# A transformer block on one core: a gate vector folded by copies, and another order for the first loads

## The chip, the cores and the metric

The kernel runs on one core of a Trainium2 chip. The metric is the device time of one execution in microseconds (us). The profile is of one execution, recorded by the hardware. In it PE is TensorE's matmul, PEld its weight load, DVE is VectorE, ACT is ScalarE, POOL is GpSimd and SP is SyncE, which here only issues DMA transfers. A q after an engine's name (SPq, ACTq) means its queue of DMA issues.

## The reference

One block of a diffusion transformer, with B = 2 sequences of N = 256 tokens, D = 1152 features and F = 4608, all in bf16. There are two heads.

```python
mod = (silu(c) @ w_mod).reshape(B, 6, 1, D)
shift_a, scale_a, gate_a, shift_m, scale_m, gate_m = [mod[:, i] for i in range(6)]
h = layernorm(x) * (1 + scale_a) + shift_a
q, k, v = split(h @ wqkv)                    # two heads of 576
a = softmax(q @ k.T * 576 ** -0.5) @ v @ wo
x = x + gate_a * a
h2 = layernorm(x) * (1 + scale_m) + shift_m
return x + gate_m * (gelu(h2 @ w_fc1) @ w_fc2)
```

## The kernel before

The 512 tokens are four tiles of 128 (t = 0 to 3). All weights are streamed from HBM in the order of their use, by SyncE. The start is a relay: c and x come in, `silu(c)` gives `sT`, x gets its statistics (ScalarE sums tiles 0 and 2, VectorE takes 1 and 3), and the normalized x is transposed on TensorE. The scale of the modulation is computed in five groups of feature blocks, each as soon as its columns of `w_mod` are there, and K is accumulated one feature block (`k_step`) at a time behind it.

```python
x_sb = act.tile([P, NT, D], BF16, name="x_sb", tag="x_sb")
nc.scalar.dma_start(c_sb[:], c_v)
nc.scalar.dma_start(touch_x[:], x_v[:, 1, 0, 0:32])
for t in (0, 1, 3, 2):
    nc.sync.dma_start(x_sb[:, t, :], x_v[:, t // TPB, t % TPB, :])
# ... constants ...
SGROUPS = [(0, 2), (2, 4), (4, 6), (6, 8), (8, 9)]
KM1 = 6

def load_k(k0, k1, c0, c1):
    nc.sync.dma_start(w_k[:, k0:k1, c0:c1], wqkv_v[:, k0:k1, D + c0:D + c1])

for k0, k1 in SGROUPS:
    nc.sync.dma_start(w_scale_a[:, :, k0 * P:k1 * P],
                      wmod_v[:, :, S_SCALE_A * D + k0 * P:S_SCALE_A * D + k1 * P])
    for a, z in [(0, 1), (1, 2)] if k0 == 0 else [(k0, k1)]:
        load_k(a, z, 0, KM1 * P)
load_k(0, KD, KM1 * P, D)
# ... then w_shift_a in two parts between the rows of w_q, w_gate_a, w_v, w_o ...
```

A scale group of two blocks is 18 narrow matmuls (128x2). The middle of the K accumulation is this loop. `transpose_x` puts block k + 1 of the normalized x into PSUM, and `both` multiplies it by the scale, the first sequence on VectorE and the second on ScalarE, into `hT0`:

```python
def both(pt, k):
    for b, e in enumerate("da"):
        modulate(pt, 0, k, b, b * N, e)

for k in range(3, KD):
    split = 2 if k in (3, 5) else 0
    k_step(k, 0, T, 0, split)              # matmuls m = 0 .. split-1 of block k
    if k in (3, 5, 7):
        k1 = min(k + 3, KD)
        scale_add(scale_group(k + 1, k1), k + 1, k1)
    if k < KD - 1:
        both(transpose_x([k + 1], range(NT)), k + 1)
    k_step(k, 0, T, split)                 # the rest of the six
```

After K come its last three panels, `shift_a` (`vec_section`), Q, the scores, V, the attention, the output projection, the second norm, the two MLP products. The last gate vector, `gate_m`, is computed on VectorE beside the first product: `part` gathers, in each of 128 partitions, the products of nine rows of `w_gate_m` with `silu(c)`. The 128 partitions must then be summed. VectorE transposes 32x32 blocks and sums them into `folded` (128 x 2 x 36). In it the four groups of 32 partitions are still separate, and the kernel before adds them with a matmul against `fold`, a matrix of four stacked identities:

```python
fold = const.tile([P, 32], FP32, name="fold")
nc.vector.tensor_reduce(fold[:], ident[:].rearrange("p (q a) -> p a q", a=32), axis=AX.X, op=ALU.add)

def gate_vector_finish(g, folded):
    rows = D // 32
    pg = aux_tile([rows, B, 32], "pg")
    for b in range(B):
        nc.tensor.matmul(pg[:, b, :], folded[:, b, :], fold[:], start=True, stop=True)
    nat = work.tile([rows, B, 32], BF16, name="nat_v", tag="nat_v", bufs=1)
    nc.vector.tensor_copy(nat[:], pg[:])
    for b in range(B):
        nc.gpsimd.dma_start(gates_dram[g, b, :].rearrange("(j r) -> j r", r=32), nat[:, b, :])
    return broadcast_gate(g)      # DRAM -> all 128 partitions, GpSimd's queue

# in the first MLP product, m = 12 .. 35, nine matmuls each
    if m == 22:
        gate_m_finish = gate_vector(1, w_gate_m)
    if m == KF - 2:
        gate_m = gate_m_finish()
```

Its first use is behind the first group of the second product, `tmp = pacc * gate_m`, whose accumulators come from a pool of six.

Of the kernel before, what the change touches and what calls it, by code (L numbers as in the profile page):

```python
# [8 lines left out]
FP32 = mybir.dt.float32  # L9
BF16 = mybir.dt.bfloat16  # L10
ACT = mybir.ActivationFunctionType
ALU = mybir.AluOpType
AX = mybir.AxisListType
# [6 lines left out]
def kernel(  # L20
# [11 lines left out]
    nc = tc.nc  # L32
    B, N, D = x.shape
# [3 lines left out]
    P = 128  # L37
    T = B * N
    NT = T // P
    TPB = N // P  # L40
    KD = D // P
    KF = F // P
# [7 lines left out]
    WAIT_FOR = mybir.DependencyInfo(mybir.DependencyClass.Sync, mybir.DependencyReason.DATA)  # L50
    first_traced = len(nc.cur_bb.bb.instructions)

    const = ctx.enter_context(tc.tile_pool(name="const", bufs=1))
    act = ctx.enter_context(tc.tile_pool(name="act", bufs=1))
    wide = ctx.enter_context(tc.tile_pool(name="wide", bufs=5))
    work = ctx.enter_context(tc.tile_pool(name="work", bufs=2))
    small = ctx.enter_context(tc.tile_pool(name="small", bufs=4))
    psum = ctx.enter_context(tc.tile_pool(name="psum", bufs=2, space=PSUM))

    def acc_tile(shape, name, dt=FP32):  # L60
        return psum.tile(shape, dt, name=name, tag="acc", bufs=6)

    def aux_tile(shape, name, dt=FP32):
        return psum.tile(shape, dt, name=name, tag="aux", bufs=2)


    x_v = x.rearrange("b (p l) d -> p b l d", l=TPB)
    out_v = out.rearrange("b (p l) d -> p b l d", l=TPB)
    c_v = c.rearrange("b (k p) -> (b k) p", p=P)
    wqkv_v = wqkv.rearrange("(k p) n -> p k n", p=P)  # L70
# [7 lines left out]
    def wide_tile(name):  # L78
        return wide.tile([P, KD, D], BF16, name=name, tag="wide")


    x_sb = act.tile([P, NT, D], BF16, name="x_sb", tag="x_sb")
# [2 lines left out]
    touch_x = act.tile([P, 32], BF16, name="touch_x")  # L85
    nc.scalar.dma_start(touch_x[:], x_v[:, 1, 0, 0:32])
    for t in (0, 1, 3, 2):
        nc.sync.dma_start(x_sb[:, t, :], x_v[:, t // TPB, t % TPB, :])  # L88

    zeros = const.tile([P, T], BF16, name="zeros")  # L90
    nc.vector.memset(zeros[:], 0.0)
    ident = const.tile([P, P], BF16, name="ident")
# [7 lines left out]
    SGROUPS = [(0, 2), (2, 4), (4, 6), (6, 8), (8, 9)]  # L100
    KM1 = 6
    w_scale_a = wide_tile("w_scale_a")
    w_k = wide_tile("w_k")

    def load_k(k0, k1, c0, c1):
        nc.sync.dma_start(w_k[:, k0:k1, c0:c1], wqkv_v[:, k0:k1, D + c0:D + c1])

    for k0, k1 in SGROUPS:
        nc.sync.dma_start(
            w_scale_a[:, :, k0 * P:k1 * P],  # L110
            wmod_v[:, :, S_SCALE_A * D + k0 * P:S_SCALE_A * D + k1 * P],
        )
        for a, z in [(0, 1), (1, 2)] if k0 == 0 else [(k0, k1)]:
            load_k(a, z, 0, KM1 * P)
    load_k(0, KD, KM1 * P, D)

    first_load = {}

    def load_rows(name, view, col0):
        w = wide_tile(name)  # L120
        for r in range(0, KD, 3):
            load = nc.sync.dma_start(w[:, r:r + 3, :], view[:, r:r + 3, col0:col0 + D])
            first_load.setdefault(name, load.ins)
        return w
# [5 lines left out]
    for (j0, j1), rows in zip(SHG, QROWS):  # L130
# [25 lines left out]
        act_func_set_id=LN_EXP_TABLES, name=nc.get_next_instruction_name(),  # L156
        engine=mybir.EngineType.Activation,
    ))
    neg_half = const.tile([P, B], FP32, name="neg_half")
    nc.gpsimd.memset(neg_half[:], -0.5)  # L160
    early = small.tile([P, 1], FP32, name="early", tag="early", bufs=1)
# [81 lines left out]
    def scale_group(k0, k1, tile_of=aux_tile, pm=None):  # L243
        if pm is None:
            pm = tile_of([P, k1 - k0, B], "pm")
        for j in range(k0, k1):
            if j == 0:
                nc.tensor.matmul(pm[:, 0, :], ones_row[:], ones_row[:, 0:B], start=True, stop=False)
            for k in range(KD):
                nc.tensor.matmul(  # L250
                    pm[:, j - k0, :], w_scale_a[:, k, j * P:(j + 1) * P], sT[:, k, 0:B],
                    start=(k == 0 and j > 0), stop=(k == KD - 1),
                )
        return pm

    def scale_add(pm, k0, k1, eng="d"):
        if eng == "a":
            nc.scalar.activation(scale_a[:, k0:k1, :], pm[:], ACT.Identity, bias=ones[:])
        else:
            nc.vector.tensor_scalar_add(scale_a[:, k0:k1, :], pm[:], 1.0)  # L260

    def transpose_x(ks, ts, pt=None, j0=0):
        if pt is None:
            pt = aux_tile([P, len(ks), len(ts) * P], "pt", BF16)
        for j, t in enumerate(ts, j0):
            for i, k in enumerate(ks):
                nc.tensor.transpose(pt[:, i, j * P:(j + 1) * P], xns[t][:, k * P:(k + 1) * P], ident[:])  # L267
        return pt
# [9 lines left out]
    def k_step(k, c0=0, c1=T, m0=0, m1=KM1):  # L278
        for m in range(m0, m1):
            if k == 0 and c0 == 0:  # L280
                pk[m] = acc_tile([P, T], "pk")
            nc.tensor.matmul(  # L282
                pk[m][:, c0:c1], w_k[:, k, m * P:(m + 1) * P], hT0[:, k, c0:c1],
                start=(k == 0 and c0 == 0), stop=(k == KD - 1), skip_group_check=True,
            )
# [33 lines left out]
# [3 lines that stand above are left out]
# [76 lines left out]
    k_step(2, 0, N)  # L398
    k_step(2, N, T)
    for k in range(3, KD):  # L400
        split = 2 if k in (3, 5) else 0
        k_step(k, 0, T, 0, split)
        if k in (3, 5, 7):
            k1 = min(k + 3, KD)
            scale_add(scale_group(k + 1, k1), k + 1, k1)
        if k < KD - 1:
            both(transpose_x([k + 1], range(NT)), k + 1)
        k_step(k, 0, T, split)
    for m in range(KM1):
        k_evac(m)  # L410

# [38 lines left out]

    s32 = const.tile([P, KD, B], FP32, name="s32")
    nc.vector.tensor_copy(s32[:], sT[:, :, 0:B])
    fold = const.tile([P, 32], FP32, name="fold")
    nc.vector.tensor_reduce(fold[:], ident[:].rearrange("p (q a) -> p a q", a=32), axis=AX.X, op=ALU.add)
    gates_dram = tc.dram_tile([2, B, D], BF16, name="gates_dram")

    def broadcast_gate(g):
        gate = act.tile([P, B, D], BF16, name="gate", tag="gate")
        for b in range(B):
            nc.gpsimd.dma_start(gate[:, b, :], gates_dram[g, b:b + 1, :].partition_broadcast(P))  # L460
        return gate
# [3 lines left out]
    def gate_vector(g, wg):  # L465
        part = act.tile([P, B, D], FP32, name="part", tag="x_sb")
        folded = small.tile([P, B, D // 32], FP32, name="folded", tag="folded", bufs=1)
        for k in range(KD):
            for b in range(B):
                if k == 0:  # L470
                    nc.vector.tensor_scalar_mul(part[:, b, :], wg[:, k, :], s32[:, k, b:b + 1])  # L471
                else:
                    nc.vector.scalar_tensor_tensor(  # L473
                        part[:, b, :], wg[:, k, :], s32[:, k, b:b + 1], part[:, b, :],
                        op0=ALU.mult, op1=ALU.add,
                    )
        for b in range(B):
            for c in range(0, D, PW):
                blocks = work.tile([P, PW // 32, 32], FP32, name="tmp", tag="tmp", bufs=3)
                nc.vector.transpose(blocks[:].rearrange("p j r -> p (j r)"), part[:, b, c:c + PW])  # L480
                nc.vector.tensor_reduce(
                    folded[:, b, c // 32:(c + PW) // 32], blocks[:], axis=AX.X, op=ALU.add
                )

        return lambda: gate_vector_finish(g, folded)

    def gate_vector_finish(g, folded):
        rows = D // 32
        pg = aux_tile([rows, B, 32], "pg")
        for b in range(B):  # L490
            nc.tensor.matmul(pg[:, b, :], folded[:, b, :], fold[:], start=True, stop=True)
        nat = work.tile([rows, B, 32], BF16, name="nat_v", tag="nat_v", bufs=1)
        nc.vector.tensor_copy(nat[:], pg[:])  # L493
        for b in range(B):
            nc.gpsimd.dma_start(gates_dram[g, b, :].rearrange("(j r) -> j r", r=32), nat[:, b, :])  # L495
        return broadcast_gate(g)

    def gate_natural(g, wg):
# [130 lines left out]
    w_gate_m = load_rows("w_gate_m", wmod_v, S_GATE_M * D)  # L629
# [118 lines left out]
    def f1_mm(dst, m, k, c0, c1, start, **kw):  # L748
        ml = m % KD
        nc.tensor.matmul(  # L750
            dst, w_f1[m // KD][:, k, ml * P:(ml + 1) * P], hT[:, k, c0:c1],
            start=start, stop=(k == KD - 1), **kw,
        )
# [23 lines left out]
    gate_m = None  # L777
    for m in range(MSPLIT, KF):
        pacc = acc_tile([P, T], "pacc")
        for k in range(KD):  # L780
            f1_mm(pacc[:], m, k, 0, T, k == 0)
        nc.scalar.activation(gT[:, m, :], pacc[:], ACT.Gelu_apprx_tanh)  # L782
        if m == 22:
            gate_m_finish = gate_vector(1, w_gate_m)
        if m == KF - 2:
            gate_m = gate_m_finish()
        if m == MSPLIT:
            load_f2(0)
        if m > MSPLIT and m % KD == KD - 1:
            load_f2(m // KD)  # L790
# [9 lines left out]
    for gi, (n, t, c0, cw) in enumerate(groups):  # L800
        b = t // TPB
        last = gi == len(groups) - 1
        pacc = acc_tile([P, cw], "pacc")
        for kk in range(KF):
            j, r = divmod(n * KF + kk, 27)
# [3 lines left out]
                start=(kk == 0), stop=(kk == KF - 1),  # L809
# [11 lines left out]
    for ins in list(nc.cur_bb.bb.instructions)[first_traced:]:  # L821
        eng = ins.engine
# [38 lines left out]
```

## Time and profile before

| what | value |
|---|---|
| time, median of three runs | 243.47 us (242.92 to 243.62) |
| span of the profiled execution | 241.3 us |
| PE busy | 236.3 us, 98% |
| PEld busy | 144.6 us, 60% |
| DVE, ACT, POOL busy | 91.6, 60.1, 28.3 us |
| HBM read | 50.15 MB, 213 GB/s over the span |
| the four loads of x, 288 KB each: issue to landing | 2.9, 3.2, 4.6, 5.1 us |
| first scale group, 576 KB: issued at, to landing | 2.57 us, 6.6 us |

The page gives busy time by engine, then the chain of work that ended last, then groups of instructions. A line of the timeline or of the chain begins with its start and its duration in us; then come the engine, the line of the kernel (L282), the operation and the tiles, and in brackets the idle time before it and what ended that. Matmuls are pipelined, so a busy PE is not a PE at its peak, and the idle time of an engine that is not the bottleneck costs nothing.

### The profile page before, as it was taken

The numbers are of one execution on the slowest core, as the hardware profiler recorded it, in microseconds if no ns is written. First come the engines' busy times: TensorE is split into PE (matmuls) and PEld (weight loads), VectorE is DVE, ScalarE is ACT, GpSimd is POOL, SyncE is SP. The second block draws the span as 40 slices with busy tenths as digits, with TensorE's granted clock in tenths as the row PEclk, the third lists the DMA queues.
The fourth block names the chain that finished last, engine by engine and source line by source line (L and its number), as shares of the span: only waits on it lengthen the run. The fifth ranks groups of instructions, "written<-read, shape, count | busy, mean of one in ns | idle before, by whom it ended". The sixth has DMA issues, their size and how long they took to land.

```text
span 241.3 us, 3993 instructions
## 1 busy us (share of the span) xinstructions
PE 236.3 (98%) x1698; PEld 144.6 (60%) x1698; DVE 91.6 (38%) x194; ACT 60.1 (25%) x122; POOL 28.3 (12%) x47
## 2 busy tenths in 40 slices
PE   8899999999999999999999999999999999999994
PEld 5675444466667566888844444444666656666674
DVE  4842442319325678930002999950000000000001
ACT  6732322307215032770423333222000000000000
POOL 2300000001400324100000000001121111111111
PEclk9999999999999999999999999999999999999999
DMA  6999999998599994739999999999300000000000
GB/s 196 324 317 311 376 367 391 389 393 249 99 315 397 387 311 81 196 62 364 390 392 392 339 326 284 285 326 275 98 16 16 20 16 16 19 18 18 26 25 16
DMA packets 48925, 53.30 MB, mean 221 GB/s; under 512 B 9731, under 2 KB 36619, under 8 KB 48907
## 3 DMA queue, kind: packets, MB, share of 16 engines
q1 hardware_dynamic: 41312, 50.14, 62.6%
q10 hardware_dynamic: 7083, 1.72, 4.9%
q0 software_dynamic: 512, 1.19, 2.2%
q8 instruction: 13, 0.21, 0.4%
q14 instruction: 5, 0.04, 0.1%
HBM read 50.15 MB, written 1.19 MB: 213 GB/s over the span
## 4 chain that ended last, share of the span: by engine, by line
PE 95%; DMA 2%; DVE 1%; SPq 0%; issue 0%; DVEq 0%
PE pacc L806 29%; PE pacc L750 29%; PE pacc L697 7%; PE pacc L603 7%; PE pq L525 7%; PE pk L282 5%; PE pk L311 2%; DMA x_sb<-in_x_dram 2%; PE pa L644 2%; PE ps_s L560 2%; PE pn L420 2%; PE pt L267 1%; PE pm L250 1%; DVE stats L195 1%; PE pg L502 0%; SPq L88 0%
## 5 line engine op out<-in xcount | busy, mean ns | idle before, releaser
L750 PE MATMUL pacc<-hT,w_f 128*128 128x256 bf16 (+1 forms) x432 | 70.5, 326 | 0.0
L806 PE MATMUL pacc<-w_f,gT 128*128 128x384 bf16 (+2 forms) x468 | 70.5, 314 | 0.0
L806 PEld LDWEIGHTS <-gT 128*128 128x128 bf16 x468 | 44.4, 98 | 26.2
L750 PEld LDWEIGHTS <-w_f 128*128 128x128 bf16 x432 | 42.2, 98 | 27.6
L812 DVE TENSOR_TENSOR tmp<-pacc,gate 128x384 f32<-128x384 f32 (+2 forms) x13 | 6.9, 527 | 65.6 <-PE pacc L806 57.3
L782 ACT ACTIVATE gT<-pacc 128x512 bf16<-128x512 f32 x24 | 14.3, 597 | 32.7 <-PE pacc L750 32.7
L473 DVE SCALAR_TENSOR_TENSOR part<-w_gate_m,s,part 128x1152 f32<-128x1152 bf16 x16 | 21.4, 1414 | 0.0
L814 POOL TENSOR_TENSOR o_sb<-tmp,x 128x384 bf16<-128x384 f32 (+1 forms) x12 | 11.6, 971 | 53.9 <-DVE tmp L812 53.9
L697 PE MATMUL pacc<-w_o,big 128*128 128x384 bf16 x108 | 17.9, 326 | 0.0
L525 PE MATMUL pq<-hT,w_q 128*128 128x512 bf16 x81 | 17.8, 379 | 0.0
L603 PE MATMUL pacc<-w_v,hT 128*128 128x384 bf16 x108 | 17.7, 326 | 0.0
L603 PEld LDWEIGHTS <-hT 128*128 128x128 bf16 x108 | 10.5, 98 | 7.1 <-issue 0.3
L697 PEld LDWEIGHTS <-big 128*128 128x128 bf16 x108 | 10.4, 98 | 7.2 <-issue 0.4
L525 PEld LDWEIGHTS <-w_q 128*128 128x128 bf16 x81 | 7.9, 98 | 9.4
L282 PE MATMUL pk<-big,w_k 128*128 128x256 bf16 (+1 forms) x72 | 13.2, 325 | 0.0
L703 POOL TENSOR_TENSOR x<-tmp,x_sb 128x384 f32<-128x384 f32 x8 | 7.3, 911 | 26.3 <-DVE tmp L702 26.3
L471 DVE TENSOR_SCALAR part<-w_gate_m,s 128x1152 f32<-128x1152 bf16 x2 | 1.6, 818 | 22.2 <-DMA w_gate_m<-in_w_mod_dram 22.2
L495 POOL DMA_DIRECT2D gates_dram<-nat_v x2 | 1.1, 534 | 67.7 <-DVE nat_v L493 67.7
L282 PEld LDWEIGHTS <-w_k 128*128 128x128 bf16 x72 | 6.8, 97 | 3.5 <-issue 0.2
L771 ACT ACTIVATE gT<-pacc 128x512 bf16<-128x512 f32 x12 | 6.5, 597 | 9.1 <-PE pacc L750 9.1
L516 POOL DMA_DIRECT2D gates_dram<-nat x4 | 2.4, 596 | 49.8 <-DVE nat L513 48.4
L175 PE MATMUL pwarm<-zeros 128*128 128x256 f32 x18 | 6.7, 540 | 1.2 <-DVE eps_t L95 1.2
(106 smaller groups left out, 164.4 us busy)
## 6 DMA issues: line engine op xcount, KB each, us to landing
w_f<-in_w_fc_dram SPq DMA_DIRECT2D x12, 864.0 KB, 14.2
w_f<-in_w_fc_dram SPq DMA_DIRECT2D x3, 1728.0 KB, 10.1
w_f<-in_w_fc_dram SPq DMA_DIRECT2D x2, 2592.0 KB, 17.2
w_gate_a<-in_w_mod_dram SPq DMA_DIRECT2D x3, 864.0 KB, 14.4
w_v<-in_wqkv_dram SPq DMA_DIRECT2D x3, 864.0 KB, 15.4
w_o<-in_wo_dram SPq DMA_DIRECT2D x3, 864.0 KB, 14.7
w_shift_m<-in_w_mod_dram SPq DMA_DIRECT2D x3, 864.0 KB, 9.5
w_scale_m<-in_w_mod_dram SPq DMA_DIRECT2D x3, 864.0 KB, 15.8
```

Source lines behind the costliest of these rows:

```text
L175: nc.tensor.matmul(dst[:, 0:T // 2], zeros32[:, 0:P], zeros32, start=True, stop=True)
L282: nc.tensor.matmul(pk[m][:, c0:c1], w_k[:, k, m * P:(m + 1) * P], hT0[:, k, c0:c1], start=(k == 0 and c0 == 0), stop=(k == KD - 1), skip_g ...
L473: nc.vector.scalar_tensor_tensor(part[:, b, :], wg[:, k, :], s32[:, k, b:b + 1], part[:, b, :], op0=ALU.mult, op1=ALU.add,)
L525: nc.tensor.matmul(pq[m][:], w_q[:, k, m * P:(m + 1) * P], hT[:, k, :], start=(k == 0), stop=(k == KD - 1), skip_group_check=True,)
L603: nc.tensor.matmul(pacc[:], hT[:, k, t * P:(t + 1) * P], w_v[:, k, pnl * PW:(pnl + 1) * PW], start=(k == 0), stop=(k == KD - 1),)
L697: nc.tensor.matmul(pacc[:], aT[:, k, t * P:(t + 1) * P], w_o[:, k, c0:c1], start=(k == 0), stop=(k == KD - 1),)
L703: (nc.gpsimd if pool_add else nc.vector).tensor_tensor(x1[:, t, c0:c1], tmp[:], x_sb[:, t, c0:c1], op=ALU.add)
L750: nc.tensor.matmul(dst, w_f1[m // KD][:, k, ml * P:(ml + 1) * P], hT[:, k, c0:c1], start=start, stop=(k == KD - 1), **kw,)
L782: nc.scalar.activation(gT[:, m, :], pacc[:], ACT.Gelu_apprx_tanh)
L806: nc.tensor.matmul(pacc[:], gT[:, kk, t * P:(t + 1) * P], w_f2[j][:, r, c0 - n * PW:c0 - n * PW + cw], start=(kk == 0), stop=(kk == KF - 1),)
L812: nc.vector.tensor_tensor(tmp[:], pacc[:], gate_m[:, b, c0:c0 + cw], op=ALU.mult)
L814: (nc.vector if last else nc.gpsimd).tensor_tensor(o_sb[:], tmp[:], x1[:, t, c0:c0 + cw], op=ALU.add)
```

## The change

There are four parts. The fold no longer uses TensorE: GpSimd's queue copies the four groups of 32 partitions of `folded` side by side into 32 partitions (`quads`), and VectorE sums, transposes and converts them. So the gate is finished as soon as it is folded and not at the next to last accumulator. In the K accumulation, three matmuls stand ahead of the second and third scale groups in place of two, so that their weights may come later, and the steps of blocks 4 and 6 are taken in halves, one sequence at a time. The first scale group's weights are issued from ScalarE's queue behind its table load, so that they travel beside x and not behind it. And row 0 of the K weights, with all that SyncE issues behind it, is held until the last load of x has landed, so that those rows don't take the DMA engines from x and the scale group.

```diff
@@ loads @@
-        nc.sync.dma_start(x_sb[:, t, :], x_v[:, t // TPB, t % TPB, :])
+        last_x = nc.sync.dma_start(x_sb[:, t, :], x_v[:, t // TPB, t % TPB, :])
...
-        nc.sync.dma_start(w_k[:, k0:k1, c0:c1], wqkv_v[:, k0:k1, D + c0:D + c1])
-
-    for k0, k1 in SGROUPS:
-        nc.sync.dma_start(
+        return nc.sync.dma_start(w_k[:, k0:k1, c0:c1], wqkv_v[:, k0:k1, D + c0:D + c1])
+
+    def load_scale(eng, k0, k1):
+        eng.dma_start(
             w_scale_a[:, :, k0 * P:k1 * P],
             wmod_v[:, :, S_SCALE_A * D + k0 * P:S_SCALE_A * D + k1 * P],
         )
+
+    for k0, k1 in SGROUPS:
+        if k0:
+            load_scale(nc.sync, k0, k1)
         for a, z in [(0, 1), (1, 2)] if k0 == 0 else [(k0, k1)]:
-            load_k(a, z, 0, KM1 * P)
+            load = load_k(a, z, 0, KM1 * P)
+            if a == 0:
+                tc.add_manual_dep(load.ins, last_x.ins.name, WAIT_FOR, reason="x first")
...
         engine=mybir.EngineType.Activation,
     ))                                       # ScalarE's table load
+    load_scale(nc.scalar, *SGROUPS[0])
@@ K accumulation @@
-        split = 2 if k in (3, 5) else 0
+        split = 3 if k in (3, 5) else 0
...
-        k_step(k, 0, T, split)
+        for c0, c1 in ((0, N), (N, T)) if k in (4, 6) else ((0, T),):
+            k_step(k, c0, c1, split)
@@ gate vector @@
-    fold = const.tile([P, 32], FP32, name="fold")
-    nc.vector.tensor_reduce(fold[:], ident[:].rearrange("p (q a) -> p a q", a=32), axis=AX.X, op=ALU.add)
...
-        pg = aux_tile([rows, B, 32], "pg")
-        for b in range(B):
-            nc.tensor.matmul(pg[:, b, :], folded[:, b, :], fold[:], start=True, stop=True)
-        nat = work.tile([rows, B, 32], BF16, name="nat_v", tag="nat_v", bufs=1)
-        nc.vector.tensor_copy(nat[:], pg[:])
-        for b in range(B):
-            nc.gpsimd.dma_start(gates_dram[g, b, :].rearrange("(j r) -> j r", r=32), nat[:, b, :])
+        quads = small.tile([32, P // 32, B * rows], FP32, name="quads", tag="quads", bufs=1)
+        for a in range(P // 32):
+            nc.gpsimd.dma_start(quads[:, a, :], folded[32 * a:32 * (a + 1), :, :].rearrange("p b j -> p (b j)"))
+        total = small.tile([32, 96], FP32, name="total", tag="total", bufs=1)
+        nc.vector.memset(total[:], 0.0)
+        nc.vector.tensor_reduce(
+            total[:, 0:B * rows], quads[:].rearrange("p a c -> p c a"), axis=AX.X, op=ALU.add,
+        )
+        turned = small.tile([32, 96], FP32, name="turned", tag="turned", bufs=1)
+        nc.vector.transpose(turned[:], total[:])
+        nat = small.tile([32, 96], BF16, name="nat_v", tag="nat_v", bufs=1)
+        nc.vector.tensor_copy(nat[:], turned[:])
+        # ... two writes to gates_dram from GpSimd's queue ...
         return broadcast_gate(g)
@@ first MLP product @@
         if m == 22:
-            gate_m_finish = gate_vector(1, w_gate_m)
-        if m == KF - 2:
-            gate_m = gate_m_finish()
+            gate_m = gate_vector(1, w_gate_m)
```

More of the change, by code (lines that the diff above doesn't have):

```diff
@@ L483, in gate_vector @@
                 )
-        return lambda: gate_vector_finish(g, folded)
-    def gate_vector_finish(g, folded):
         rows = D // 32
-        pg = aux_tile([rows, B, 32], "pg")
-        for b in range(B):
-            nc.tensor.matmul(pg[:, b, :], folded[:, b, :], fold[:], start=True, stop=True)
-        nat = work.tile([rows, B, 32], BF16, name="nat_v", tag="nat_v", bufs=1)
-        nc.vector.tensor_copy(nat[:], pg[:])
-        for b in range(B):
-            nc.gpsimd.dma_start(gates_dram[g, b, :].rearrange("(j r) -> j r", r=32), nat[:, b, :])
+        quads = small.tile([32, P // 32, B * rows], FP32, name="quads", tag="quads", bufs=1)
[10 more added lines that the diff above has]
+        nc.vector.tensor_copy(nat[:], turned[:])
+        flat = gates_dram[g, :, :].rearrange("b (j r) -> (b j) r", r=32)
+        nc.gpsimd.dma_start(
+            flat[0:64, :].rearrange("(q c) r -> c q r", q=2), nat[:, 0:64].rearrange("c (q r) -> c q r", q=2),
+        )
+        nc.gpsimd.dma_start(flat[64:B * rows, :], nat[0:B * rows - 64, 64:96])
         return broadcast_gate(g)
```

## The prediction

> **What bounds the kernel now.** I read first the page's busy shares, then the chain of waits that ended last (whole, then cut to the first 35 us), then the timeline of the two stretches that the change touches, then the DMA issues one at a time with their times to landing.
>
> The page says TensorE is busy 98% of the span, and the chain says 95% of the end is set by it. So a change counts only where it removes TensorE work, or where TensorE waits. The first place is the fold of the last gate vector. The chain has it as a piece of its own, between matmuls of the first MLP product:
>
> ```profile
> 97.31 68.26 PE pacc L750 x423
> 165.57 0.26 PE pg L491 x4
> 165.82 2.05 PE pacc L750 x9
> 167.87 70.31 PE pacc L806 x468
> ```
>
> The reader is to see that the four fold matmuls stand in the chain, and that the nine matmuls behind them took 2.05 us. The same stretch on ScalarE shows the rhythm of the accumulators around it:
>
> ```profile
> 163.66 0.60 ACT L782 ACTIVATE gT<-pacc 128x512 bf16<-128x512 f32 x1 [1.34 <-PE pacc L750]
> 165.61 0.60 ACT L782 ACTIVATE gT<-pacc 128x512 bf16<-128x512 f32 x1 [1.35 <-PE pacc L750]
> 167.91 0.60 ACT L782 ACTIVATE gT<-pacc 128x512 bf16<-128x512 f32 x1 [1.71 <-PE pacc L750]
> ```
>
> The first column is the start. One accumulator follows another by 1.95 us (163.66 to 165.61), and the one with the fold in it by 2.30 us.
>
> The second place is the start. Here TensorE waits for x, for the norm, and then runs beside the loads. From the chain of the first 35 us:
>
> ```profile
> 1.63 4.60 DMA x_sb<-in_x_dram
> 6.23 0.02 issue
> 6.25 1.49 DVE stats L195 x3
> ...
> 7.92 0.68 DVE xn L235 x2
> 8.60 0.04 issue
> 8.64 0.62 PE pt L267 x8
> ```
>
> The third of the four loads of x lands at 6.23 us, VectorE takes its statistics at once, normalizes, and TensorE starts its useful work at 8.64. The fourth quarter was issued at 2.06 and took 5.1 us to land, 7.2 us; ScalarE starts its statistics of it at 7.23. So both late quarters of x sit on the path with nothing to spare. What the DMA engines did in this time, in stretches (the last two columns are their busy share and the GB/s):
>
> ```profile
> 0.70:1.70 1.00, 0.52 (x1) 0.50 (x2) 0.28 (x2) 0.00 (x0) 0.82 (x4) 1.00 0.00 0
> 1.70:4.50 2.80, 2.80 (x8) 1.79 (x7) 0.73 (x4) 2.35 (x3) 0.76 (x3) 1.00 0.96 299
> 4.50:6.00 1.50, 1.50 (x5) 1.17 (x4) 1.47 (x4) 1.47 (x3) 0.00 (x0) 1.00 0.84 227
> 6.00:9.00 3.00, 2.30 (x16) 1.72 (x15) 2.65 (x9) 2.73 (x8) 1.30 (x4) 1.00 1.07 325
> ```
>
> For one microsecond after the first issue nothing moves; then the engines are full but for a hole of 16% of 1.5 us at 4.5 to 6.0. After that TensorE and the loads run neck and neck. Two scale groups come just late:
>
> ```profile
> 15.37 0.57 PEld L250 LDWEIGHTS <-w_scale_a 128*128 128x128 bf16 x18 [0.26 <-DMA w_scale_a<-in_w_mod_dram]
> 19.09 0.52 PEld L250 LDWEIGHTS <-w_scale_a 128*128 128x128 bf16 x18 [0.45 <-DMA w_scale_a<-in_w_mod_dram]
> ```
>
> These idle times are of the weight loads. In the chain the second group took 0.56 us where the first two took 0.43, so TensorE itself lost about 0.13 us there, and hardly anything at 15.4. That is all that a smoother supply of scale groups could give.
>
> **What the Trainium skill says.** "DMA: Bandwidth & Descriptors", section "Issuing engines are not separate DMA queues": transfers from several issuing engines run on the same 16 DMA engines and interleave; a second issuer saves only issue time. The trace of before can't show it, since its ScalarE queue carries only two tiny loads there, but its busy share of 0.96 and above says there is little idle time to take. The same page, "Queues, rings and completion order": each DMA engine takes turns between the queues that have work. If so, x and the first scale group share the engines in the changed kernel, where before the group stood behind x in one queue. "Perfetto Trace Analysis", section "Per-instruction lifecycle": the recorded time of a DMA instruction is that of its descriptors and not of the data. Before agrees: x is issued in some 0.4 us a quarter and lands after 2.9 to 5.1. "VectorE: DVE Perf Modes", section "Why `tensor_reduce` can't reduce along partition axis": lanes don't exchange data. That is why the new fold needs copies before its reduction; no run yet shows it.
>
> **The change, part by part.**
>
> Fold by copies. It removes four matmul records (0.26 us) from TensorE's chain, and the nine matmuls behind them stop paying for the switch: 2.05 us against the usual 1.95. Together 2.30 - 1.95 = 0.35, or 0.26 + 0.10 = 0.36. I take -0.36. In their place VectorE and the GpSimd queue do the work. The last block of the vector is folded at 159.86 + 0.55 = 160.4. Four copies are issued at some 0.55 us each (the old writes of the vector took 1.06 for two) to 162.6 and land some 3 us later (the old writes took 3.7 to land), 165.6; four small VectorE operations take about 1 us; the two writes to DRAM another 4.2; the broadcast 4.3. Estimate: the gate is there at about 175, where it came at 174.40. The first output group is finished near 173.3, and with six accumulators of 5.4 us each TensorE can go on for some 30 us without it. So nothing of this shows in the time. The dropped reduction that made the fold matrix (0.36 us of VectorE at 32.8) lies off the path: 0.
>
> Later scale groups and halves. The split of 3 moves one matmul of 0.215 us (0.86 for four) ahead of each of two scale groups: no work more, and 0.2 us more time for the load. It would recover the 0.13, if the loads were as punctual as before. The halves turn 12 matmuls of 512 columns into 24 of 256. The chain has 18 of 256 and two of 512 in 2.41 us, so one of 256 takes (2.41 - 0.43)/18 = 0.110, and a pair 0.220 for 0.215: 12 x 0.005 = +0.06. What they buy is that the first half needs only VectorE's product; it makes up for the matmul that no longer stands between the scale group and this step.
>
> First scale group from ScalarE's queue, row 0 held. The group (576 KB) was issued at 2.57 and landed at 9.17, and TensorE took it at 9.3. So it was just in time, and earlier is worth nothing, as TensorE waits at 8.64 for the norm of x. What it costs: from the moment that its pieces of 512 B flow, they take turns with rows of 2304 B of x, and x has 2304/2816 = 82% of the engines. If they flow from about 3.6 us, x still has 1.18 MB - 1.9 x 0.299 = 0.61 MB to go. It took from 3.6 to 6.2 and 7.2 for its last two quarters; 22% longer is +0.6, less the hole of 0.16 x 1.5 = 0.24 us that it fills. I take +0.35 us on the late quarters of x. These stand on the path, so TensorE starts later, or waits at 11.08 for the last quarter's norm.
>
> Then the hold. Row 0 of K is issued only when x is in, say at 7.55. From the first issue of x to its landing in an empty queue took 2.9 us for 288 KB, so 192 KB should land after some 2.5 us, near 10.05. TensorE took row 0 at 10.13, which becomes about 10.5 with the later x: row 0 makes it. What comes behind is less sure. With 1 us before anything moves, the engines can run dry once x and the first group (1.77 MB) are through, near 7.5, until about 8.5. That is 0.3 MB not moved at 325 GB/s, less 0.08 MB won in the old hole. Much of it is idle time of those DMA engines that had run ahead, and a landing waits for the slowest, so I put the delay of later loads at 0.3 us, which lies beside the +0.35 of x and is not added to it. I take +0.40 for the start, of which the later groups give back 0.05.
>
> Sum: 243.47 - 0.36 + 0.06 + 0.40 - 0.05 = 243.52.
>
> **The rivals.**
>
> 1. The hold costs nothing and x is not disturbed: the hole at 4.5 to 6.0 is filled, all loads come a little earlier. For it: the 227 GB/s there, and that the group's load on its own queue does not wait behind the slowest part of x. Against it: the engines are full before and after, and TensorE's start hangs on x alone. Then the time is 243.47 - 0.36 + 0.06 - 0.19 = 242.98, about 243.0; it can hardly be less.
> 2. The loads become the bound: the dry microsecond is never made up, since the engines run at a share of 1.07 to 1.13 up to 29 us, and every later group comes 0.7 to 1.0 us late. The load of shift_a (issued 18.36, landed 28.8, used at 29.2) has about 0.4 us in hand, the scale groups less. Then the start costs 0.7 to 1.0 and the time is 243.9 to 244.2.
> 3. The issue on ScalarE delays its first exponential. ScalarE is idle until 3.41 us, its table load ends at 3.05, and an issue takes 0.4 to 0.6. If the sequencer issues only after the table is loaded, the silu, and with it VectorE's full queue, starts 0.2 us later; but then the group also disturbs x later. About the same sum.
> 4. The gate comes so late by the longer detour that the output waits. It would need 30 us; I leave it at nothing.
>
> **Range and chances.** The sure part is -0.36. The start lies between -0.19 and +1.0, and the three runs before spread over 0.7 us. I predict 243.5 us, and 242.7 to 244.3 should hold it 8 times in 10. Two per cent are 4.9 us, far beyond either end: same 0.97, faster 0.01, slower 0.02.
>
> **What would show it.** Right: no fold matmul in the chain, and the accumulators at that place all 1.95 us apart; the late quarters of x landing 0.2 to 0.6 us later than 6.23 and 7.2, and the first transposes or the wait at 11.08 moved by as much; the first scale group landing well before 9; a dip in the GB/s at 7.5 to 8.5; row 0 of K landing near 10. Wrong: x landing as before or earlier, or its late quarters no longer the last thing that VectorE and ScalarE wait for; waits of 0.7 us and more for scale groups or for shift_a (rival 2); the first output groups held by the gate past 180 us.

## The result and the profile after

The changed kernel takes 247.0 us (median of 6 runs, 245.42 to 247.78), the kernel before took 243.69 in the same comparison. The ratio is 1.0128, with a 95% interval of 1.0088 to 1.0169. So the change costs some 3 us, and the range of the prediction (242.7 to 244.3) does not hold it. The profiled execution of the changed kernel has a span of 243.6 us, against 241.3 before: 2.3 us are to be found in it.

The chain of waits of the changed kernel begins thus (start, duration, what):

```profile
2.10 6.49 DMA x_sb<-in_x_dram
8.59 0.02 issue
8.61 0.33 SPq L106
...
9.46 0.43 SPq L109
...
13.97 8.07 DMA w_scale_a<-in_w_mod_dram
22.04 0.05 issue
22.09 0.60 PE pm L257 x18
```

Before, the chain went from the third quarter of x to VectorE and then stayed on TensorE. Now it goes from the fourth quarter of x, which lands at 8.59 us and not at 7.2, to SyncE's queue, which is released by it (row 0 of K at 8.61, the second scale group at 9.46), and through the queue to the landing of the fourth scale group at 22.04. TensorE joins the chain only then. The start is bound by the loads.

What the DMA engines did, in stretches (the last two columns are busy share and GB/s):

```profile
1.70:4.50 2.80, 2.80 (x8) 1.79 (x7) 0.68 (x3) 2.19 (x3) 0.76 (x3) 1.00 0.89 294
4.50:6.00 1.50, 1.50 (x5) 1.16 (x4) 1.42 (x3) 1.47 (x3) 0.00 (x0) 1.00 1.01 280
6.00:7.00 1.00, 1.00 (x4) 0.80 (x3) 0.31 (x3) 0.79 (x4) 0.48 (x2) 1.00 1.04 343
7.00:8.00 1.00, 1.00 (x6) 0.90 (x5) 0.99 (x3) 0.40 (x3) 0.00 (x0) 1.00 0.49 166
8.00:9.00 1.00, 0.46 (x3) 0.06 (x1) 0.97 (x5) 0.38 (x1) 0.15 (x1) 1.00 0.10 31
9.00:10.00 1.00, 0.60 (x9) 0.51 (x9) 0.34 (x3) 0.97 (x3) 0.69 (x2) 1.00 0.35 45
10.00:12.00 2.00, 2.00 (x33) 1.51 (x32) 1.31 (x6) 1.88 (x5) 0.57 (x2) 1.00 0.81 233
```

The same stretches of the kernel before:

```profile
7.00:8.00 1.00, 0.95 (x5) 0.49 (x3) 0.97 (x4) 0.97 (x3) 0.00 (x0) 1.00 1.07 300
8.00:9.00 1.00, 0.35 (x7) 0.36 (x8) 0.75 (x4) 0.97 (x3) 0.82 (x2) 1.00 1.09 360
9.00:10.00 1.00, 1.00 (x29) 0.88 (x27) 0.69 (x3) 0.96 (x2) 0.60 (x3) 1.00 1.12 329
10.00:12.00 2.00, 1.99 (x20) 1.45 (x18) 1.68 (x8) 0.96 (x4) 0.00 (x0) 1.00 1.12 316
```

The hole at 4.5 to 6.0 is filled as the change meant it (280 for 227 GB/s). Behind it the engines run dry: 166, 31 and 45 GB/s where the kernel before moved 300, 360 and 329, and 233 for 316 in the two microseconds after that. From 7 to 10 us alone that is (989 - 242) x 1 us = 0.75 MB not moved, or 2.3 us at 325 GB/s.

Where TensorE pays, from its timeline (in brackets the idle time ahead, and what ended it):

```profile
9.39 0.62 PE L274 MATMUL pt<-ident,xn 128*128 128x128 bf16 x8 [0.93 <-DVE xn L242]
12.46 0.29 PE L274 MATMUL pt<-ident,xn 128*128 128x128 bf16 x2 [0.40 <-DVE xn L242]
14.86 0.60 PE L257 MATMUL pt<-sT,w_scale_a 128*128 128x2 bf16 x18 [0.85 <-DMA w_scale_a<-in_w_mod_dram]
22.09 0.60 PE L257 MATMUL pm<-sT,w_scale_a 128*128 128x2 bf16 x18 [0.33 <-DMA w_scale_a<-in_w_mod_dram]
```

The same four stood at 8.64, 11.08, 12.47 and 19.10 before; there the second scale group was not waited for:

```profile
12.47 0.59 PE L250 MATMUL pt<-sT,w_scale_a 128*128 128x2 bf16 x18
```

The delay grows from 0.75 (third quarter of x) to 1.38 (fourth quarter) to 2.39 (second scale group) to 2.99, of which 0.2 is the one matmul that now stands ahead. The first matmuls of shift_a come at 31.97 for 29.23: 2.74 us late. From there both kernels run alike up to the fold:

```profile
166.41 0.60 ACT L795 ACTIVATE gT<-pacc 128x512 bf16<-128x512 f32 x1 [1.35 <-PE pacc L763]
168.35 0.60 ACT L795 ACTIVATE gT<-pacc 128x512 bf16<-128x512 f32 x1 [1.35 <-PE pacc L763]
170.29 0.60 ACT L795 ACTIVATE gT<-pacc 128x512 bf16<-128x512 f32 x1 [1.34 <-PE pacc L763]
```

The accumulators are all 1.94 us apart. The 2.30 us of the one with the fold in it are gone, 0.36 us are won, and the second MLP product begins 2.38 us late (170.25 for 167.87), which is the difference of the spans. The gate comes at 177.86 for 174.40, and no matmul waits for it.

### The profile page after: what moved, and what is told of

Same layout as the page of the kernel before. It is cut to its first block, busy times and chain, and to the rows that moved or that the text cites. A ratio compares the mean times of both kernels' runs of the same rounds, so it can differ in the third digit from the quotient of the medians.

```text
span 243.6 us, 4006 instructions
## 1 busy us (share of the span) xinstructions
PE 236.3 (97%) x1695; PEld 145.8 (60%) x1706; DVE 92.2 (38%) x196; ACT 60.1 (25%) x122; POOL 30.2 (12%) x51
## 4 chain that ended last, share of the span: by engine, by line
PE 89%; DMA 6%; SPq 3%; issue 0%; DVE 0%; DVEq 0%
PE pacc L817 29%; PE pacc L763 29%; PE pacc L710 7%; PE pacc L616 7%; PE pq L538 7%; DMA w_scale_a<-in_w_mod_dram 3%; DMA x_sb<-in_x_dram 3%; PE pk L318 2%; PE pk L289 2%; SPq L106 2%; PE pa L657 2%; PE ps_s L573 2%; PE pn L428 2%; SPq L88 1%; PE pg L515 0%
## 5 line engine op out<-in xcount | busy, mean ns | idle before, releaser
L494 POOL DMA_DIRECT2D quads<-folded x4 | 2.0, 507 | 62.1 <-DVE total L496 62.1
L289 PEld LDWEIGHTS <-w_k 128*128 128x128 bf16 x84 | 7.8, 98 | 2.7 <-DMA w_k<-in_wqkv_dram 0.2
L182 PE MATMUL pwarm<-zeros 128*128 128x256 f32 x18 | 7.2, 574 | 1.2 <-DVE eps_t L95 1.2
```

Of the source, the lines that this page charges most:

```text
L182: nc.tensor.matmul(dst[:, 0:T // 2], zeros32[:, 0:P], zeros32, start=True, stop=True)
L289: nc.tensor.matmul(pk[m][:, c0:c1], w_k[:, k, m * P:(m + 1) * P], hT0[:, k, c0:c1], start=(k == 0 and c0 == 0), stop=(k == KD - 1), skip_g ...
```

## The experiments

The theory after this profile: ScalarE issues the scale group at 1.81 us, between the third (1.63) and the fourth (2.10) quarter of x. What is issued first is moved first, so the fourth quarter stands behind the group's rows. The hold then keeps everything else back until that quarter is in, and the DMA engines run dry. The rivals: the hold alone is the cost; or the sharing of the engines by two queues is.

| run | what it is | us, median (n) | ratio to before, interval |
|---|---|---|---|
| e4 | new fold alone | 243.19 (22) | 0.999, 0.9979 to 1.0001 |
| e3 | new fold, later groups and halves | 243.07 (22) | 0.9981, 0.9971 to 0.9990 |
| e6 | e3 + hold until the second quarter of x | 243.03 (12) | 0.9985, 0.9968 to 1.0001 |
| e5 | e3 + group from ScalarE behind x, no hold | 244.62 (11) | 1.0057, 1.0036 to 1.0079 |
| e9 | e3 + group ahead of x's last quarter, one queue | 245.4 (4) | 1.0086, 1.0066 to 1.0107 |
| e2 | e3 + hold | 245.73 (4) | 1.0083, 1.0055 to 1.0112 |
| e11 | e2 once more | 245.51 (6) | 1.0077, 1.0048 to 1.0106 |
| e10 | e2, TensorE's waits filled | 244.95 (6) | 1.0062, 1.0043 to 1.0081 |
| e1 | e3 + group from ScalarE, no hold | 246.63 (4) | 1.0131, 1.0105 to 1.0158 |
| e7 | changed kernel, waits filled | 246.4 (5) | 1.0127, 1.0103 to 1.0151 |
| e12 | changed kernel once more | 246.71 (4) | 1.0141, 1.0106 to 1.0175 |
| e8 | changed kernel, x's last two quarters swapped | 246.32 (1) | one run |

Many of these times hold one more effect, a stretch at half TensorE clock in some of the runs, which the last group of experiments takes apart.

**e1: the changed kernel without the hold.**

```diff
-            load = load_k(a, z, 0, KM1 * P)
-            if a == 0:
-                tc.add_manual_dep(load.ins, last_x.ins.name, WAIT_FOR, reason="x first")
+            load_k(a, z, 0, KM1 * P)
```

> The changed kernel without the hold: K row 0 is issued right behind x, the first scale group still from ScalarE's queue. Theory (order of issue: the last quarter of x, issued at 2.10, stands behind the scale group, issued at 1.81, and the hold then keeps everything else back until it is in): the last quarter of x still lands near 8.5 us, but the DMA engines no longer run dry between 7.5 and 9.5, the second scale group is no longer waited for, and about half of the loss comes back: 244.3 us (243.9 to 244.8). Rival A (the hold is the whole cost): x as late as it is does no harm, 243.1. Rival B (sharing the engines with the scale group is the cost, and the hold protected x): without the hold x lands later still, past 9, and the time is 246 or more.

246.63 us: my theory's 244.3 was missed, and what Rival B said came. On TensorE's timeline of this run:

```profile
10.13 0.62 PE L272 MATMUL pt<-ident,xn 128*128 128x128 bf16 x8 [2.44 <-DVE xn L240]
11.96 0.61 PE L255 MATMUL pm<-sT,w_scale_a 128*128 128x2 bf16 x18 [1.11 <-DMA w_scale_a<-in_w_mod_dram]
```

The third quarter of x took 6.1 us to land and the fourth 7.2 (7.7 and 9.3 us), later than with the hold, so TensorE starts at 10.13. The group itself took 10.1 us, to 11.9; TensorE waits 1.11 us for it. The GB/s show no dry stretch: 325, 338 and 339 from 7 to 10. So the hold did protect the group from the rows of K: in the four profiles with the hold and the group on its own queue it took 7.4 to 8.5 us. For x that is not shown, since one of these four (e7) has it as late as here (7.9 and 9.2 us). The hold is not the whole cost (Rival A falls). All four runs of e1 had the lowered clock (0.986 to 0.993), so its 3.2 us are not of the loads alone.

**e2: the hold without the other queue.** The group is back on SyncE's queue, behind x.

```diff
-        if k0:
-            load_scale(nc.sync, k0, k1)
+        load_scale(nc.sync, k0, k1)
...
-    load_scale(nc.scalar, *SGROUPS[0])
```

> The changed kernel with the first scale group back on SyncE's queue behind x; K row 0 still held until x is in. Theory: x lands as in the kernel before (6.2 and 7.2 us), the hold is released at 7.2 and the engines are dry for a shorter time, since the scale group is still under way; later loads 0.5 to 1.0 us late: 243.5 to 244.2. Rival A (the hold is the whole cost): 245 or more. Rival B (the sharing is the whole cost): 243.1.

245.73 us, where I expected 243.5 to 244.2; 245 or more was Rival A's number. The stretches of this run:

```profile
6.00:7.00 1.00, 1.00 (x5) 0.83 (x4) 1.00 (x4) 0.84 (x4) 0.48 (x2) 1.00 1.13 340
7.00:8.00 1.00, 1.00 (x6) 0.69 (x4) 0.97 (x4) 0.83 (x3) 0.05 (x1) 1.00 0.53 155
8.00:9.00 1.00, 0.66 (x9) 0.45 (x8) 0.63 (x4) 0.97 (x3) 0.79 (x2) 1.00 0.54 144
9.00:10.00 1.00, 1.00 (x27) 0.88 (x25) 0.72 (x4) 1.00 (x2) 0.58 (x2) 1.00 0.93 293
10.00:12.00 2.00, 1.76 (x16) 1.20 (x14) 1.37 (x7) 0.92 (x6) 0.00 (x0) 1.00 0.91 230
```

x is in time (5.3 us for the last quarter, to 7.4), and TensorE starts at 8.51. But the engines drop to 155 and 144 GB/s, and once more to 230 behind the two rows of K. TensorE pays mainly at one place:

```profile
14.75 0.60 PE L255 MATMUL pt<-sT,w_scale_a 128*128 128x2 bf16 x18 [1.92 <-DMA w_scale_a<-in_w_mod_dram]
```

The second scale group was issued at 8.29 in place of 4.80 and took 6.4 us to land. So either part of the change alone costs over 2 us, with the clock of some runs in it, and both together little more than the group alone. The two delays hide each other: TensorE gets to the second scale group at 14.75 with the hold alone and at 14.86 with both, so the later x is spent inside the wait for the group.

**e3 and e4: the other parts.** e3 is e2 without the hold; e4 also takes back the split and the halves.

```diff
-        split = 3 if k in (3, 5) else 0
+        split = 2 if k in (3, 5) else 0
...
-        for c0, c1 in ((0, N), (N, T)) if k in (4, 6) else ((0, T),):
-            k_step(k, c0, c1, split)
+        k_step(k, 0, T, split)
```

> Only the fold by copies, the later scale groups and the halves; the loads are those of the kernel before. All theories: start as before, shift_a's first matmuls at 29.2 us, no fold in TensorE's chain, -0.36 for the fold and 0 to -0.1 for the groups: 243.1 to 243.3. If the time stays at that of before, the fold's gain is given back elsewhere.

> Only the fold by copies. -0.36 us for TensorE's missing fold: 243.1 to 243.3, the same as with the later groups within 0.1 us.

The times are as expected, within their intervals: the fold alone 0.999, that is -0.24 us with an interval of -0.5 to 0, which just reaches no gain at all, and with the later groups 0.9981, -0.46 us (-0.7 to -0.24). The 0.12 us between the two medians are less than they are uncertain. e3 is clear of both the kernel before and the changed one: the version to keep. Its profile is of its slowest execution (243.97 us) and misses the expected start of shift_a, 30.48 for 29.2: the first and the fourth scale group were waited for by some 0.7 us each, with the loads of the kernel before. So much the loads vary by themselves.

**e5: the group behind x.** The question was whether the order of issue or the second queue delays x. One more small load on ScalarE's queue shifts the group's issue; the trace has it at 2.66 us, 0.5 us behind the last quarter of x. There is no hold.

```diff
     nc.scalar.dma_start(touch_x[:], x_v[:, 1, 0, 0:32])
+    touch_more = act.tile([P, 32], BF16, name="touch_more")
+    nc.scalar.dma_start(touch_more[:], x_v[:, 1, 0, 32:64])
```

> The changed kernel without the hold, and with one more small load (64 bytes a partition) ahead of the first scale group on ScalarE's queue, so that the group is issued near 3.1 us, behind the last quarter of x (2.10) and not ahead of it (1.81). Theory (order of issue decides): the last two quarters of x land near 6.2 and 7.2 again, not at 7.7 and 9.3 as in the run without the hold, and the time is 243.1 to 243.9. Rival (two queues sharing the engines slow x, whatever the order): x at 8 us or later and 245 or more.

244.62 us: neither. The third quarter is early (4.2 us to land, at 5.8), the fourth at 8.0, between the two. In the seven profiles whose group stands behind x on SyncE's queue the fourth lands at 6.7 to 7.7 us; in the five with the group issued ahead from ScalarE's queue, at 8.6 to 9.3. And a new wait takes over, on TensorE's timeline:

```profile
11.15 0.60 PE L257 MATMUL pm<-sT,w_scale_a 128*128 128x2 bf16 x18 [1.68 <-DMA w_scale_a<-in_w_mod_dram]
```

The group, issued at 2.66 on its own queue, is there at 11.1; before, issued at 2.57 behind x in one queue, it landed at 9.17 (9.9 in e3's profile). Beside it the rows of K come from SyncE's queue and take their share, where in one queue they stand behind it.

**e9: the order without a second queue.** All loads on SyncE's queue, no hold, and only the place of the group changed, ahead of x's last quarter.

```diff
-    for t in (0, 1, 3, 2):
+    for t in (0, 1, 3):
...
         load_scale(nc.sync, k0, k1)
+        if k0 == 0:
+            nc.sync.dma_start(x_sb[:, 2, :], x_v[:, 1, 0, :])
```

> The kernel with the new fold and the later groups, all loads on SyncE's queue, no hold; only the first scale group is issued ahead of the last quarter of x. Theory (what is issued first is moved first; the second queue is not what counts for x): the last quarter lands at 8.3 to 9.0 us, the third as before; TensorE waits for the last quarter's norm near 12.4; 244.0 to 244.7. Rival (only a second queue can delay x): last quarter at 7.2 and 243.1.

On ScalarE's timeline of this run, the statistics of that quarter:

```profile
9.65 1.25 ACT L213 ACTIVATE sink<-x_sb 128x1152 f32<-128x1152 bf16 x1 [2.46 <-DMA x_sb<-in_x_dram]
```

The last quarter, issued at 2.57, took 7.1 us and landed at 9.7. That is even later than I said, and the time, 245.4 us, is above the expected 244.0 to 244.7, with a part of it in the clock (below). Order within one queue is enough to delay x; no second queue is needed. What order means between two queues this run can't say.

**e8: which quarter is late.** In the changed kernel the last two quarters of x are issued in the other order.

```diff
-    for t in (0, 1, 3, 2):
+    for t in (0, 1, 2, 3):
```

> The changed kernel with the last two quarters of x issued in the other order (tile 2 third, tile 3 fourth). Theory (the fourth issue stands behind the scale group's rows): whatever tile is issued third lands near 6.9 us, and the fourth near 8.6. Rival (the tile's own rows are slow): tile 2 keeps landing at 8.6.

The third and the fourth load of x in this run (last column: us to landing):

```profile
x_sb<-in_x_dram SPq DMA_DIRECT2D x1, 288.0 KB, 3.8
x_sb<-in_x_dram SPq DMA_DIRECT2D x1, 288.0 KB, 6.7
```

Tile 2, now third, is in at 1.63 + 3.8 = 5.4; tile 3, now fourth, at 2.10 + 6.7 = 8.8. In the changed kernel it was 5.3 and 6.5 us for tiles 3 and 2. So it is the place in the order, not the tile. The third quarter came earlier than the expected 6.9: it isn't late in every run.

The single transfers of the changed kernel show how far the order goes. From 4.5 to 5.5 us 438 transfers of ScalarE's queue begin, the group's rows of 512 B, and 41 of SyncE's; from 5.0 to 5.5 none of x. From 5.5 to 8.5 both move together, 712 and 151. So the group goes ahead for a microsecond and then the two share the engines. It is not served whole before x: the quarter issued behind it lands at 8.6, the group at 9.3.

**e6: a shorter hold.** e2 with the hold on the second quarter of x, which lands at 4.4 us.

```diff
+        if t == 1:
+            last_x = load_x
```

> The hold alone, as before, but until the second quarter of x is in (near 4.4 us) in place of the last (7.4). Theory (the hold costs because the DMA engines run dry): with the scale group and half of x still queued at 4.4 they don't run dry; no dip in the GB/s at 7 to 9, no wait of 1.9 us for the second scale group, 243.1 to 243.6. Rival (any wait in front of row 0 breaks the stream, or the order itself): 244.5 or more.

243.03 us, as expected. The stretches in which e2 was dry:

```profile
7.00:8.00 1.00, 1.00 (x6) 0.88 (x5) 0.97 (x4) 0.97 (x3) 0.00 (x0) 1.00 1.14 320
8.00:9.00 1.00, 0.89 (x10) 0.49 (x9) 0.71 (x3) 0.97 (x3) 0.86 (x3) 1.00 1.07 367
```

Here a wait in front of row 0 cost nothing, as the engines still had work when it ended. Released at 4.4 there were half of x and a scale group left, released at 7.4 next to nothing.

**e7, e10, e11, e12: the clock.** The runs of the changed kernel fall apart: three, of the first comparison and of e12, took 245.42, 245.46 and 245.64 us at a mean granted TensorE clock of 0.998 to 1.000, the other seven 246.17 to 248.26 at 0.991 to 0.993. e10 fills the waits of e2 with matmuls of zeros, e7 those of the changed kernel.

```diff
+    def fill_k(n):
+        for _ in range(n):
+            nc.tensor.matmul(pk[0][:, 0:N], zeros[:, 0:P], zeros[:, 0:N], start=False, stop=False, skip_group_check=True)
...
+    fill_k(4)
     transpose_x([0, 1], [2], pt_c, 0)
...
+    fill_k(15)                    # e7: 8; warm-up 7 -> 8, e7: 10
     scale_group(2, 4, pm=pm)
```

> The changed kernel with TensorE kept busy in its three waits: three more warm-up matmuls, and 4 and 8 matmuls of zeros, which add nothing to the accumulator, ahead of the last quarter's transposes and of the second scale group. Theory on the clock (the runs of the changed kernel fall into 245.4 us at a mean granted clock of 0.998 and 246.8 to 247.8 at 0.992, which is one stretch of 3.4 us at half clock after the waits): all runs at 0.997 or more, and 245.2 to 245.8. Rival (the spread is of the loads): 246.5 to 247.5, as without the fill.

> The hold alone (first scale group on SyncE's queue), with TensorE's waits filled by matmuls of zeros: one more warm-up, 4 ahead of the last quarter's transposes, 15 ahead of the second scale group, where TensorE waited 1.9 us. Theory on the clock (a wait of some 2 us lets the clock fall to half for 3.4 us in some of the runs, which costs about 1 us): every run at 0.998 or more and 244.8 to 245.4, no run at 246. Rival (the spread is of the loads): runs up to 246.1 at full clock.

> The hold alone once more, unfilled, beside the filled one. Theory on the clock: two groups of runs, near 245.0 at 0.998 to 1.000, and near 246.1 at 0.991 to 0.993. Rival: no link of time and clock.

> The changed kernel once more. Theory: 245.4 to 247.8; the runs with a granted clock near 0.992 are the slow half, those at 0.998 or more the fast half; x lands late (third quarter near 7, last past 8.5), and the hold is released then.

The hold alone in e11, unfilled, by stretches (the column before the last two is the granted clock), and TensorE behind the wait:

```profile
12.00:14.00 2.00, 0.62 (x6) 0.30 (x4) 0.46 (x2) 0.26 (x1) 0.00 (x0) 1.00 1.06 318
14.50:17.90 3.40, 3.40 (x33) 2.60 (x34) 1.49 (x5) 0.84 (x2) 0.00 (x0) 0.50 1.13 325
18.00:20.00 2.00, 2.00 (x32) 1.47 (x31) 0.16 (x1) 0.00 (x0) 0.00 (x0) 1.00 1.14 299
```

```profile
14.47 0.64 PE L255 MATMUL pt<-sT,w_scale_a 128*128 128x2 bf16 x18 [1.86 <-DMA w_scale_a<-in_w_mod_dram]
15.14 4.13 PE L287 MATMUL pk<-big,w_k 128*128 128x256 bf16 x21
```

And filled, in e10, the same stretch and the same 21 matmuls:

```profile
14.50:17.90 3.40, 3.40 (x44) 2.60 (x41) 1.48 (x5) 0.84 (x2) 0.00 (x0) 1.00 1.12 323
```

```profile
15.17 2.79 PE L287 MATMUL pk<-big,w_k 128*128 128x256 bf16 x21
```

After a wait of 1.86 us the clock stands at half for one stretch of 3.4 us, and 21 matmuls take 4.13 us for 2.79. In e11 the three runs at 0.991 took 245.94 to 246.28 us, the three at 0.998 or more 243.96 to 245.08: 1.6 us between the means, near the 1.7 us that half of 3.4 can cost. With the waits filled, all runs of e10 and e7 have 0.998 or more. So the clock follows from the waits, and filling them keeps it up. The Trainium skill has this: "TensorE: Matmul & The Clock Gate", section "Part 1: The HAM clock gate", says that a monitor with free-running windows of about 3.4 us halves the clock after an idle window, and calls the warm-up run-variable. The trace agrees with its 3.41 us and its half; here a wait of 1.9 us was enough in half of the runs.

Why only in half can be read from the clock records of the profiles. The clock changes only at whole multiples of 3.41 us after its first rise, and that rise comes at another time in each run (4.5 to 7.7 us). Five profiles have a fall (e1, e5, e8, e9, e11). In each it comes 6.83 us after the rise, and TensorE's waits in the 3.41 us ahead of it add up to 1.68 us (e5) to 3.31 us (e8). In the nine profiles without a fall no such stretch holds more than 1.63 us (e12). In e11 the wait of 1.86 us lies whole in one stretch, 11.08 to 14.49; in e2 the wait of 1.92 us is cut at 13.35 into 0.52 and 1.40, and the clock stays. The fourteen profiles fit this, but no run moved a wait on purpose.

Filling did not bring all the time back, and that part of my expectation failed: one run of e10 took 246.25 at full clock, and e7 stayed at 246.0 to 247.2, above the 245.5 of the changed kernel's runs at full clock. In e7's profile the last quarter of x landed at 9.2, later than in any profile of the changed kernel. There TensorE still waits 0.49 and 0.70 us for scale groups behind the fill, so in this execution the loads are late and not the fill long. Why they are later than in the changed kernel stays open. e12 ran up to 248.26 us, above the expected 247.8.

## Why the prediction was wrong

- **The fold, -0.36: right** in the trace (1.94 us apart, 0.36 won) and on the chip within its interval. The gate came at 177.9 and not at 175 because the fold itself ended late, at 163.25 for 160.4. From there the detour took 14.6 us, as estimated, though its parts differ: 7.4 us to VectorE's sum for 5.2, 1.9 for the writes to DRAM for 4.2. The slack of 30 us held it, as said. The reason given for the copies was too wide: VectorE's transposes do move data between partitions, in blocks of 32 (`STREAM_TRANSPOSE`, the last at 162.1 us). Only the four groups of 32 stay apart.
- **Halves and later groups, +0.06 and -0.05: not refuted**; the runs give -0.12, inside the noise.
- **The late quarters of x, +0.35: the mechanism half right, the term mis-sized.** I let the group take turns with x from 3.6 us on, row by row, so that x would keep 82% of the engines. The group's rows begin at 4.5 us, have the engines almost alone for a microsecond, and then x moves 0.31 MB of 0.67 from 5.5 to 8.5 us, less than half. Measured +0.7 on the third and +1.39 on the fourth quarter, and the wait at 12.46 came as described. The group gained nothing by it: issued 0.76 us sooner, it landed at 9.3 for 9.17, where I had expected it well before 9.
- **The hold, 0.3 us "beside the +0.35 of x": the step that failed.** I allowed 0.3 MB not moved and then argued most of it away, since a landing waits for the slowest DMA engine. It was 0.75 MB from 7 to 10 us, and e2 shows the hold alone costing 2.3 us (245.73 against 243.39), in the same comparison in which e3 was at 243.07. Half of e2's runs had the lowered clock; the five runs of e2 and e11 at 0.998 or more have a mean of 244.7, which still is 1.4 us. Three things were missing. x landed later, so the release came at 8.6 and not at 7.55. After the release the first row of K took 2.4 us, to 11.0; I had that duration, but from too early a start, and TensorE's weight load did wait for it, by 0.2 us. And the queue does not fill at once: two rows of K (192 KB each) keep the engines busy for barely more than a microsecond, and the scale group behind them flows only later. Hence the second dip to 230 or 233 GB/s, and a second scale group 2.4 us late.
- **"Not added to it": right in form.** The group alone costs 3.2 us (every run with the lowered clock), the hold alone 2.3, both 3.3 to 3.5. But the larger of the two was not 0.40.
- **Rival 2 named the right mechanism** (dry engines, later scale groups late, shift_a behind them), and gave it 0.7 to 1.0 us; the profile has 2.74. I gave it too little weight, although the hold's purpose was to stop a stream that ran at 96% and more.
- **Rival 3 fell:** the group is issued at 1.81, while the table load runs (1.78 to 3.06), and the first exponential starts at 3.40 as before.
- **Not foreseen: the clock.** TensorE's waits let it fall to half in seven of the ten runs of the changed kernel, and these seven are 1.8 us slower in the mean than the other three. Without it the change costs about 2 us; with it, 3.3. The filled runs (e7) kept the clock and still took 246.0 us and more, so not all of the 1.8 is shown to be the clock's.

## What to carry to other kernels

Before holding a load back, count the bytes that are still queued when it is released: e6 and e2 differ only in that, and by 2.6 us, each against its own runs of the kernel before (some of it the clock in half of e2's runs). A second queue does not put a load "beside" another for nothing: the two share the engines. Here the load that was moved came no earlier (9.3 us for 9.17), and x came 1.4 us later. And a kernel whose TensorE is barely covered by its loads pays a wait of 2 us twice, once as the wait and once, in some of its runs, in the clock.

## What was not expected of the hardware

- A load issued from ScalarE's queue delays a later issue from SyncE's, though each has its own queue: 6.5 us to landing for 5.1. The Trainium skill's "DMA: Bandwidth & Descriptors", section "Issuing engines are not separate DMA queues", says only that they interleave; the trace adds that the turns are not even: 438 transfers against 41 in one microsecond, then 712 against 151 in three.
- Restarting a dry stream is dear: 2.4 us for 192 KB issued into empty engines, and less than half speed for a microsecond behind it (128 GB/s at 11 to 12 us, 334 before) while the next 576 KB in rows of 512 B begin.
- ScalarE's sequencer issues a DMA during its own table load: 1.81 us, inside 1.78 to 3.06.
- The granted clock fell after a single wait of 1.9 us, for 3.41 us, in about half of the runs of the same kernel; in the fourteen profiles it fell where 1.68 us or more of waiting lay inside one of its stretches of 3.41 us, and held where it was 1.63 or less.
